# Linear attention: the queries' products taken one head at a time over 64 rows, instead of two heads at once through a block-diagonal matrix

## Chip, core and metric

The kernel runs on one core of a Trainium2 chip. The metric is the device time of one execution in microseconds (us); of the kernel before, the median of three runs is 1168.2 us. Names of engines in the rows: PE is TensorE's products, PEld its loads of the fixed operand ("weights"), DVE is VectorE, ACT is ScalarE, POOL is GpSimd, SPq the queue on which SyncE issues transfers.

## What is computed

```python
# attention: batch 4, heads 8, sequence 576, head size 64, all float32
q_s = softmax(q over the head size)          # per query
k_s = softmax(k over the sequence)           # per column of a head
kv  = einsum('bhsd,bhse->bhde', k_s, v)      # one 64 x 64 matrix per batch and head
x   = einsum('bhsd,bhde->bhse', q_s, kv)     # 2304 tokens of 8 x 64 = 512
# first mixture: 8 experts, each token goes to one, 288 tokens per expert, best logits first
logits = x @ w_gate                          # 512 -> 8
...                                          # greedy assignment, then relu(x @ w1[e]) @ w2[e]
# second mixture: 4 experts, all tokens through all, weighted by normalised domain_probs
out += p[:, e:e+1] * (relu(x @ w1[e]) @ w2[e])
```

## The kernel before

The program has three stages. The first, some 93 us, is the attention with the gate's logits. The second searches for one expert after the other which 288 tokens it takes, gathers them from `x_rows` in memory and runs them through the expert; the third is the second mixture. In each stage the calls are collected in a `Plan`; every engine's instructions are then issued in an order that the plan works out from prices (`price`, L107), from the dependences and from a priority (L190 to L197). On the chip each engine runs its list in that order and waits where an operand is not ready. An engine never passes over an instruction that waits.

The attention stage has 8 steps `kv_half` (L588: a batch and four of its eight heads) and 18 chunks of 128 queries: 16 from `q_half` (L655), whose queries are of one batch, and 2 from `q_rest` (L662), of which each holds the last 64 queries of two batches. The order of the steps stands in `ATT["order"]` (L67).

`kv_half` adds up in the PSUM tile `pkv` the products of exp(k) and v for pairs of heads; head `h` of a pair goes to partitions 64h to 64h+63, and a 65th column holds the column sum. DVE divides and writes the two heads into `mov`, a matrix of 128 rows and 146 columns for each pair: head 0 in rows 0 to 63 and columns 0 to 63, head 1 in rows 64 to 127 and columns 64 to 127, zeros beside them, two columns of ones that give the queries' sums, and 16 columns for the gate. For the gate's columns the block is transposed into the tile `pg`, copied to `kvT` by ACT, multiplied by `wg` (the gate's weights) and copied back into `mov` by DVE.

`q_cols` (L617) transposes a chunk's queries (tile `pa`, four transposes), takes exp of them (`qT`, ACT), and multiplies each pair's 128 columns of `qT` by that pair's `mov`:

```python
xp = aps("pkv", [P, 2, 512], F32, 2).rearrange("p a (b c) -> p (a b) c", b=2)
for p in range(NP):
    for rs, b in parts:
        pl.tensor.matmul(xp[rs, p, :146], qT[:, p, rs], mov[b][:, p], start=True, stop=True)
```

The first operand of `matmul` behind the output is the fixed one (a load of weights), the second is streamed through it. The results are divided by the sums (`rq`), the gate's part is added to `logits`, and the 512 outputs (`xo`) go to `x_rows`, on DVE straight from PSUM or, by `ATT["x"]`, copied by ACT (`xr`) and multiplied on POOL.

After the last chunk, the first search (`search`, L339) reads `logits`, and the second stage goes on from there.

Of the kernel before, what the change touches and what calls it, by code (L numbers as in the profile page):

```python
# [8 lines left out]
F32 = mybir.dt.float32  # L9
# [4 lines left out]
AF = mybir.ActivationFunctionType  # L14
# [11 lines left out]
SM = P * NI  # L26
SR = S - SM
NC = NT // P

DL = (650.0, 1300.0, 330.0, 1900.0)  # L30
GRP = ((0, 12), (12, 18))
# [57 lines left out]
class Plan:  # L89
# [16 lines left out]
    @staticmethod  # L106
    def price(key, name, out, ins):  # L107
        n = 1
        for c in out.shape[1:]:
            n *= c  # L110
        m = n
        for i in ins:
            c = 1
            for d in i.shape[1:]:
                c *= d
            m = max(m, c)
        if "dma" in name:
            return (1000.0 if key == "POOL" else 60.0, 4 * n * out.shape[0])
        if key == "PE":
            if name == "transpose":  # L120
                return 110.0
            d = ins[1].dtype
            if d == F32:
                return 85.0 if n == D + 1 else max(n, 128) * 1.7 if n >= 96 else 213.0
            if d == F32R:
                return n / 2.4 + 3
            return max(27.0, n / 2.4 + 3)
        if key == "DVE":
            if name == "tensor_reduce":
                return 70 + 1.04 * m  # L130
            if name == "tensor_scalar" or name == "tensor_copy":
                rate = 0.52 if str(ins[0].space).endswith("SB") and str(out.space).endswith("SB") else 1.04
                return 68 + rate * n + (60 if len(ins) > 1 else 0)
            rate = 0.52 if out.dtype == BF and name == "tensor_tensor" else 1.04
            return 69 + (60 if name == "scalar_tensor_tensor" and len(ins) > 2 else 0) + rate * n
        if key == "ACT":
            return 55 + 0.835 * n
        if key == "POOL":
            if name == "tensor_tensor":
                return 155 + 2.1 * n  # L140
            return 180 + 1.05 * n
        return 60.0
# [99 lines left out]
def block_kernel(ctx, tc, q, k, v, w_gate, m1_w1, m1_w2, probs, m2_w1, m2_w2, out):  # L242
# [19 lines left out]
    nc.gpsimd.iota(dpc, pattern=[[1, P]], base=0, channel_multiplier=-1)  # L262
    ident = const.tile([P, P], F32, name="ident")
    nc.vector.tensor_scalar(ident, dpc, 0.0, None, op0=OP.is_equal)
    wg = const.tile([P, NP, E1], F32, name="wg")
    logits = const.tile([P, NC, E1], F32, name="logits")

    pl = Plan(nc)
# [201 lines left out]
    with ExitStack() as at:  # L470
# [22 lines left out]
        for nm, bp in (("k", 0), ("v", 0), ("q", 0), ("k", 1), ("v", 1), ("q", 1)):  # L493
            src = {"k": k, "v": v, "q": q}[nm]
            for b in (2 * bp, 2 * bp + 1):
                load_main(nm, src, b, 2 if nm == "k" and b == 0 else 1)
                if b == 2 * bp:
                    load_rest(nm, src, bp)
            if bp == 0 and nm == "v":
                pl.sync.dma_start(wg, w_gate.rearrange("(c p) e -> p c e", p=P))  # L500
        for b in range(B):
            pl.sync.dma_start(pr[:, b * NI:(b + 1) * NI], probs[b * S:b * S + SM].rearrange("(r i) e -> r i e", i=NI))
            s = b % 2
# [6 lines left out]
            pl.gpsimd.memset(va[(1 - s) * SR:(2 - s) * SR, NI], 0.0)  # L510
            vaug.append(va)
        for b in range(B):
            mov[b] = kt_(f"mov{b}", [P, NP, 146])
            pl.gpsimd.memset(mov[b], 0.0)
            for s in range(2):
                pl.gpsimd.memset(mov[b][s * D:(s + 1) * D, :, 128 + s:129 + s], 1.0)
        ps = kt_("ps", [P, NC])
        px = kt_("px", [P, NC, EX])
        HH = H // 2
# [62 lines left out]
        def guard(o, t, way):  # L582
            if way:
                pl.scalar.activation(o, t, AF.Copy, bias=EPS)
            else:
                pl.vector.tensor_scalar(o, t, EPS, None, op0=OP.add)

        def kv_half(bp, u, s):  # L588
            b = 2 * bp + s
            kx, ke, va = tiles["k", "x", bp], kt_(f"ke{s}", [P, NI, H, D]), vaug[s]  # L590
            kv = aps("pkv", [P, 2, 512], F32, 2)[:, 0, :HP * (D + 1)].rearrange("p (a c) -> p a c", a=HP)
            for j in range(HP):
                for i in range(NI + 1):
                    for h in range(2):
                        n = 2 * (u * HP + j) + h
                        w = ke[:, i, n] if i < NI else kx[:, n]
                        pl.tensor.matmul(kv[h * D:(h + 1) * D, j], w, va[:, i, n], start=(i == 0), stop=(i == NI))
            rs = kt_("rs", [P, HP, 1], F32, 2)
            guard(rs, kv[:, :, D:], ATT["g"][0])
            pl.vector.reciprocal(rs, rs)  # L600
            mv = mov[b][:, u * HP:(u + 1) * HP]
            for h in range(2):
                hp = slice(h * D, (h + 1) * D)
                pl.vector.tensor_tensor(mv[hp, :, hp], kv[hp, :, :D], rs[hp].to_broadcast([D, HP, D]), op=OP.mult)
            tp = aps("pg", [P, 512])
            for j in range(HP):
                pl.tensor.transpose(tp[:, j * P:(j + 1) * P], mv[:, j, :P], ident)
            kvT = kt_("kvT", [P, HP, P], F32, 2)
            pl.scalar.activation(kvT, tp[:, :HP * P].rearrange("p (a b) -> p a b", a=HP), AF.Copy)
            g = tp[:, 384:384 + HP * E1].rearrange("p (a e) -> p a e", a=HP)  # L610
            for j in range(HP):
                pl.tensor.matmul(g[:, j], kvT[:, j], wg[:, u * HP + j], start=True, stop=True)
            for h in range(2):
                hp = slice(h * D, (h + 1) * D)
                pl.vector.tensor_copy(mv[hp, :, 130 + 8 * h:138 + 8 * h], g[hp])

        def q_cols(qt, c, parts):  # L617

# [2 lines left out]
                pl.tensor.transpose(tp[:, p], qt[:, 2 * p:2 * p + 2, :], ident)  # L621
            qT = kt_("qT", [P, NP, P], F32, 2)
            pl.scalar.activation(qT, tp, AF.Exp)
            xp = aps("pkv", [P, 2, 512], F32, 2).rearrange("p a (b c) -> p (a b) c", b=2)
            for p in range(NP):
                for rs, b in parts:
                    pl.tensor.matmul(xp[rs, p, :146], qT[:, p, rs], mov[b][:, p], start=True, stop=True)
            rq = kt_("rq", [P, NP, 2], F32, 2)
            guard(rq, xp[:, :, 128:130], ATT["g"][1])
            pl.vector.reciprocal(rq, rq)  # L630
            lp = kt_("lp", [P, NP, 2, E1], F32, 2)
            pl.vector.tensor_tensor(lp, xp[:, :, 130:146].rearrange("p a (h e) -> p a h e", h=2),
                                    rq[:, :, :, None].to_broadcast([P, NP, 2, E1]), op=OP.mult)
            xo = kt_("xo", [P, DX], F32, 3)
            eng, xv = pl.vector, xp[:, :, :P]
            if ATT["x"][c]:
                xr = kt_("xr", [P, NP, P], F32, 2)
                pl.scalar.activation(xr, xv, AF.Copy)
                eng, xv = pl.gpsimd, xr
            eng.tensor_tensor(xo[:, :DM].rearrange("p (a h d) -> p a h d", a=NP, h=2),  # L640
                              xv.rearrange("p a (h d) -> p a h d", h=2),
                              rq[:, :, :, None].to_broadcast([P, NP, 2, D]), op=OP.mult)
            pl.vector.tensor_reduce(logits[:, c], lp.rearrange("p a h e -> p e (a h)"), axis=AX.X, op=OP.add)
            pl.scalar.activation(xo[:, DM:], px[:, c], AF.Copy)
# [391 lines left out]
```

## Time and profile before

| what | value |
|---|---|
| three runs | 1166.06, 1168.2, 1171.34 us (median 1168.2) |
| the profiled execution | 1172.77 us, of which its span (first to last instruction) is 1170.9 us |
| TensorE's products, busy | 1099.8 us, 94% of the span |
| DVE, ACT, POOL, busy | 713.1, 470.9 and 500.1 us |
| mean granted TensorE clock | 0.977 of full speed |

The three runs lie within 0.45% of each other, and the profiled execution is 0.4% above their median. A busy share is an average over stages with different limits, so the stage of the change has to be looked at by itself. A product of two float32 operands leaves two records in the trace, each with a load of its own; a transpose on TensorE leaves one. A record's duration goes from its start to its modelled end and overlaps the next one, so what a product costs the engine is read from the distance between records.

### The profile page before, as it was taken

The page shows a single profiled execution, that of the slowest core. Times are in us where ns is not written, and L with a number is a line of the kernel's source. Part 1 is how long each engine was busy: PE and PEld are TensorE (multiplying, and loading weights), DVE is VectorE, ACT ScalarE, POOL GpSimd, SP SyncE. Part 2 cuts the span into 40 slices and gives each one's busy share as a digit, 9 for nine tenths or more (in the row PEclk, how much of TensorE's full clock was granted, in tenths as well). Part 3 has the DMA queues.
Part 4 walks back from the last instruction along what each step waited for, and adds up shares of the span by engine and source line. Part 5 has one row for each costly group of instructions (what it writes and reads, how often), then busy time and mean ns, then how long its engine had stood idle before and what let it go on. Part 6 is the DMA issues. An engine that isn't in the chain of part 4 may idle for free.

```text
span 1170.9 us, 20079 instructions
## 1 busy us (share of the span) xinstructions
PE 1099.8 (94%) x7708; PEld 989.4 (84%) x7708; DVE 713.1 (61%) x1700; ACT 470.9 (40%) x945; POOL 500.1 (43%) x645
## 2 busy tenths in 40 slices
PE   4783999999999899999999999999999999999996
PEld 2673888999989899889989898798899898888995
DVE  5977575877744565555555559755555555555553
ACT  3451354645556543333434344433333333333321
POOL 5462111211121666555455555945344343444222
PEclk9896798999999999999999999999999999999998
DMA  9922686877788512111111112202111111110001
GB/s 278 236 92 87 168 241 155 218 203 189 204 229 222 155 38 72 55 54 37 55 54 55 55 37 72 89 24 69 36 37 37 55 36 36 54 38 18 1 37 54
DMA packets 81760, 113.64 MB, mean 97 GB/s; under 512 B 11520, under 2 KB 56576, under 8 KB 81664
## 3 DMA queue, kind: packets, MB, share of 16 engines
q1 hardware_dynamic: 74080, 86.09, 24.1%
q0 software_dynamic: 7584, 26.27, 10.2%
q8 instruction: 60, 0.98, 0.3%
q14 instruction: 36, 0.29, 0.1%
HBM read 86.08 MB, written 9.48 MB: 82 GB/s over the span
## 4 chain that ended last, share of the span: by engine, by line
PE 79%; DVE 7%; DMA 5%; issue 4%; POOL 3%; ACT 1%; SPq 0%; DVEq 0%; POOLq 0%; ACTq 0%
PE o L85 31%; PE x L85 16%; PE z L85 8%; PE y L85 7%; PE hp L85 7%; PE q L85 4%; DMA w<-raw 2%; DMA xg<-x_rows,idx 2%; PE pkv L85 2%; PE sm L85 2%; PE tp L85 1%; PE pm L85 1%; DVE yops L85 1%; POOL w L85 1%; DMA k<-in_k 1%
## 5 line engine op out<-in xcount | busy, mean ns | idle before, releaser
L85 PE MATMUL o<-w,h 128*128 128x512 f32 x1728 | 534.8, 394 | 4.4 <-DVE h L85 2.8
L85 PEld LDWEIGHTS o<-w,h 128*128 128x128 f32 x1728 | 311.1, 188 | 48.4 <-DVE h L85 4.2
L85 PE MATMUL x<-yops,w 128*128 128x256 f32 (+1 forms) x1536 | 342.9, 295 | 0.6 <-ACT yops L85 0.6
L85 POOL TENSOR_TENSOR w<-raw,w 128x256 fp32r<-128x256 f32 x224 | 171.4, 795 | 312.9 <-ACT w L85 267.7
L85 DVE SCALAR_TENSOR_TENSOR y<-o,prs,y 128x512 f32<-128x512 f32 x270 | 198.7, 748 | 142.6 <-PE o L85 140.0
L85 PEld LDWEIGHTS x<-yops,w 128*128 128x128 f32 x1536 | 262.6, 188 | 21.6 <-ACT yops L85 0.8
L85 ACT ACTIVATE w<-raw 128x1024 fp32r<-128x1024 f32 (+2 forms) x192 | 166.2, 878 | 192.6 <-PE q L85 66.8
L85 PE MATMUL z<-yops,w 128*128 128x256 f32 (+1 forms) x768 | 178.3, 295 | 0.7 <-DVE mid L85 0.7
L85 ACT ACTIVATE mid<-x 128x256 f32<-128x256 f32 (+1 forms) x192 | 78.0, 408 | 206.0 <-PE x L85 203.9
L85 DVE SCALAR_TENSOR_TENSOR h<-mid,h 128x256 fp32r<-128x256 f32 (+1 forms) x192 | 117.1, 610 | 64.7 <-ACT h L85 64.4
L85 ACT ACTIVATE h<-mid 128x256 fp32r<-128x256 f32 (+1 forms) x192 | 84.6, 441 | 139.6 <-DVE mid L85 139.4
L85 PEld LDWEIGHTS z<-yops,w 128*128 128x128 f32 x768 | 132.9, 189 | 5.8 <-DVE mid L85 0.9
L85 PE MATMUL y<-h,w 128*128 128x288 f32 x768 | 127.6, 306 | 1.5 <-DMA w<-raw 0.9
L85 PE MATMUL hp<-xT,w 128*128 128x288 f32 x768 | 126.6, 306 | 0.4 <-ACT xT L85 0.4
L85 PEld LDWEIGHTS y<-h,w 128*128 128x128 f32 x768 | 109.1, 192 | 3.6 <-DMA w<-raw 1.8
L85 POOL DMA_DIRECT2D w<-raw x32 | 28.9, 903 | 192.4 <-ACT h L85 81.9
L85 PEld LDWEIGHTS hp<-xT,w 128*128 128x128 f32 x768 | 109.4, 193 | 1.8 <-ACT xT L85 0.6
L85 POOL TENSOR_TENSOR w<-sums,w 128x256 fp32r<-128x256 f32 x128 | 100.5, 821 | 23.1 <-ACT w L85 23.1
L85 PE MATMUL q<-yops,w 128*128 128x256 f32 (+1 forms) x384 | 102.5, 295 | 0.0
L85 PEld LDWEIGHTS q<-yops,w 128*128 128x128 f32 x384 | 70.8, 188 | 7.5
L85 DVE TENSOR_TENSOR mid<-mid,z 128x256 f32<-128x256 f32 (+1 forms) x128 | 57.6, 450 | 30.1 <-PE z L85 17.5
L85 DVE TENSOR_TENSOR mid<-mid,q 128x256 f32<-128x256 f32 (+1 forms) x64 | 29.0, 453 | 53.5 <-PE q L85 46.4
(198 smaller groups left out, 1011.4 us busy)
## 6 DMA issues: line engine op xcount, KB each, us to landing
raw<-in_moe_w SPq DMA_DIRECT2D x128, 512.0 KB, 3.8
w<-raw POOLq DMA_DIRECT2D x32, 512.0 KB, 5.8
x_rows<-xo SPq DMA_DIRECT2D x16, 258.5 KB, 2.4
v<-in_v SPq DMA_DIRECT2D x4, 1024.0 KB, 9.6
q<-in_q SPq DMA_DIRECT2D x4, 1024.0 KB, 11.1
k<-in_k SPq DMA_DIRECT2D x3, 1024.0 KB, 9.6
k<-in_k SPq DMA_DIRECT2D x2, 512.0 KB, 6.0
x_rows<-xo SPq DMA_DIRECT2D x4, 129.2 KB, 2.7
```

Of the source, the lines that this page charges most:

```text
L85: lambda: getattr(self.engine, name)(*args, **kw), ins, out, kw.get("start", True))
```

## The change

One head's product now has 64 rows of its own on both sides. `mov` keeps, for each pair of heads, head 0 in rows 0 to 63 and head 1 in rows 64 to 127 of the same 73 columns (64 of the head, one of ones, eight of the gate); the zeros are gone. In `q_cols` each pair is two products of 64 contracted rows and 73 columns; those of head 0 go to one PSUM bank, those of head 1 to the other. In `kv_half` one DVE instruction over 128 partitions takes the place of two over 64, in the division and in the copy of the gate's columns. The block is transposed from 64 columns, so `kvT` has 64 partitions, and the gate's product is two products of 64 by 64. `wg` is laid out with 64 rows. `price` gives the new products 85 ns each, as it gave those of `kv_half`.

```diff
 NC = NT // P
+QC = D + 1 + 8
...
-                return 85.0 if n == D + 1 else max(n, 128) * 1.7 if n >= 96 else 213.0
+                return 85.0 if n == D + 1 or n == QC and ins[0].shape[0] == D else max(n, 128) * 1.7 if n >= 96 else 213.0
...
-    wg = const.tile([P, NP, E1], F32, name="wg")
+    wg = const.tile([D, H, E1], F32, name="wg")
...
-                pl.sync.dma_start(wg, w_gate.rearrange("(c p) e -> p c e", p=P))
+                pl.sync.dma_start(wg, w_gate.rearrange("(h d) e -> d h e", d=D))
...
-            mov[b] = kt_(f"mov{b}", [P, NP, 146])
-            pl.gpsimd.memset(mov[b], 0.0)
-            for s in range(2):
-                pl.gpsimd.memset(mov[b][s * D:(s + 1) * D, :, 128 + s:129 + s], 1.0)
+            mov[b] = kt_(f"mov{b}", [P, NP, QC])
+            pl.gpsimd.memset(mov[b][:, :, D:D + 1], 1.0)
...
-            for h in range(2):
-                hp = slice(h * D, (h + 1) * D)
-                pl.vector.tensor_tensor(mv[hp, :, hp], kv[hp, :, :D], rs[hp].to_broadcast([D, HP, D]), op=OP.mult)
+            pl.vector.tensor_tensor(mv[:, :, :D], kv[:, :, :D], rs.to_broadcast([P, HP, D]), op=OP.mult)
             tp = aps("pg", [P, 512])
             for j in range(HP):
-                pl.tensor.transpose(tp[:, j * P:(j + 1) * P], mv[:, j, :P], ident)
-            kvT = kt_("kvT", [P, HP, P], F32, 2)
-            pl.scalar.activation(kvT, tp[:, :HP * P].rearrange("p (a b) -> p a b", a=HP), AF.Copy)
+                pl.tensor.transpose(tp[:D, j * P:(j + 1) * P], mv[:, j, :D], ident)
+            kvT = kt_("kvT", [D, HP, P], F32, 2)
+            pl.scalar.activation(kvT, tp[:D, :HP * P].rearrange("p (a b) -> p a b", a=HP), AF.Copy)
             g = tp[:, 384:384 + HP * E1].rearrange("p (a e) -> p a e", a=HP)
             for j in range(HP):
-                pl.tensor.matmul(g[:, j], kvT[:, j], wg[:, u * HP + j], start=True, stop=True)
-            for h in range(2):
-                hp = slice(h * D, (h + 1) * D)
-                pl.vector.tensor_copy(mv[hp, :, 130 + 8 * h:138 + 8 * h], g[hp])
+                for h in range(2):
+                    hp = slice(h * D, (h + 1) * D)
+                    pl.tensor.matmul(g[hp, j], kvT[:, j, hp], wg[:, 2 * (u * HP + j) + h], start=True, stop=True)
+            pl.vector.tensor_copy(mv[:, :, D + 1:], g)
...
-            xp = aps("pkv", [P, 2, 512], F32, 2).rearrange("p a (b c) -> p (a b) c", b=2)
+            xp = aps("pkv", [P, 2, 512], F32, 2)[:, :, :NP * QC].rearrange("p h (a c) -> p a h c", a=NP)
             for p in range(NP):
                 for rs, b in parts:
-                    pl.tensor.matmul(xp[rs, p, :146], qT[:, p, rs], mov[b][:, p], start=True, stop=True)
+                    for h in range(2):
+                        hp = slice(h * D, (h + 1) * D)
+                        pl.tensor.matmul(xp[rs, p, h], qT[hp, p, rs], mov[b][hp, p], start=True, stop=True)
```

The reads of `xp` behind these lines (`rq`, `lp`, `xr`, `xo`) follow the new layout with as many elements as before.

Since prices and pieces differ, the plan issues the attention stage in another order. From the first search on, all engines have the same order as before. A product uses a part of TensorE's array: by the rows that it contracts (128, or half of them) and by the partitions that it writes (128, or half of them). In what follows this is the shape of a product, and going from one shape to another a switch. A transpose of 64 columns writes 64 partitions, so it has the shape of the products in `kv_half`. In the stage before, from its first product to the first search, PE's list has 41 switches between two shapes (128 rows to 128 partitions, 128 rows to 64), the last one into the search; in the changed one it has 86, between four shapes. The rows below are of PE's list: output, streamed operand and fixed operand, then partitions and columns of the output, and how many stand in a row.

First place: PE's last chunks ahead of the first search, before.

```order
L85 MATMUL pa_147<-ident,qe_157 128x128
L85 MATMUL pkv_137<-mov_0_122,qT_148 128x146 x4
L85 MATMUL pa_147<-ident,qe_157 128x128 x3
L85 MATMUL pkv_141<-mov_0_122,qT_153 128x146 x4
L85 MATMUL pa_152<-ident,qe_157 128x128 x4
L85 MATMUL pkv_137<-mov_0_123,qT_148 128x146 x4
L85 MATMUL pkv_141<-mov_0_123,qT_153 128x146 x4
```

Here all rows have one shape: transposes (`pa`) and products (`pkv`) use the whole array. The same place after the change:

```order
L86 MATMUL pa_152<-ident,qe_145 128x128 x4
L86 MATMUL pkv_137<-mov_0_123,qT_148 128x73 x8
L86 MATMUL pkv_141<-mov_0_123,qT_153 128x73 x8
L86 MATMUL pa_147<-ident,qe_157 128x128 x4
L86 MATMUL pkv_137<-mov_0_122,qT_148 128x73 x8
L86 MATMUL pa_152<-ident,qe_157 128x128 x4
L86 MATMUL pkv_141<-mov_0_122,qT_153 128x73 x8
L86 MATMUL pkv_137<-mov_0_123,qT_148 128x73 x8
L86 MATMUL pkv_141<-mov_0_123,qT_153 128x73 x8
```

Each group of products of 128x73 contracts 64 rows, so it has a shape of its own: these nine rows have five switches where the seven rows above have none, and three chunks stand at the end without a transpose between them, where there were two.

Second place: PE's list around the last `kv_half`, whose block is transposed (`pg<-ident`) and multiplied by the gate's weights (`pg<-wg`), before.

```order
L85 MATMUL pg_139<-ident,mov_0_123 128x128 x2
L85 MATMUL pkv_141<-mov_0_122,qT_153 128x146 x4
L85 MATMUL pkv_137<-mov_0_122,qT_148 128x146 x4
L85 MATMUL pa_152<-ident,qe_145 128x128 x4
L85 MATMUL pg_139<-wg,kvT_143 128x8
L85 MATMUL pa_147<-ident,qe_157 128x128 x4
L85 MATMUL pg_139<-wg,kvT_143 128x8
L85 MATMUL pkv_141<-mov_0_122,qT_153 64x146
```

Until the last row, where a rest chunk begins, nothing switches. The same place after the change:

```order
L86 MATMUL pg_139<-ident,mov_0_123 64x128 x2
L86 MATMUL pa_152<-ident,qe_145 128x128 x3
L86 MATMUL pkv_141<-mov_0_122,qT_153 128x73 x8
L86 MATMUL pa_152<-ident,qe_145 128x128
L86 MATMUL pa_147<-ident,qe_157 128x128 x3
L86 MATMUL pg_139<-wg,kvT_143 64x8 x2
L86 MATMUL pkv_137<-mov_0_122,qT_148 128x73 x8
L86 MATMUL pa_147<-ident,qe_157 128x128
L86 MATMUL pg_139<-wg,kvT_143 64x8 x2
L86 MATMUL pkv_141<-mov_0_122,qT_153 64x73 x2
```

The gate's products (64 rows to 64 partitions) now stand between transposes of the whole array and chunks of 64 rows, and there are seven switches where there was one.

## Rows read from the trace of the kernel before

**Rows 1.** The page: span, and part 1 (busy us, share of the span, instructions).
```profile
span 1170.9 us, 20079 instructions
PE 1099.8 (94%) x7708; PEld 989.4 (84%) x7708; DVE 713.1 (61%) x1700; ACT 470.9 (40%) x945; POOL 500.1 (43%) x645
```

**Rows 2.** Busy time by stretch: span, engines (instructions), granted clock, DMA share, GB/s.
```profile
20.00:60.00 40.00, 32.63 (x361) 27.26 (x361) 35.33 (x79) 19.58 (x47) 19.53 (x17) 0.91 0.95 237
60.00:91.00 31.00, 26.46 (x269) 23.16 (x268) 25.02 (x77) 17.98 (x56) 20.28 (x16) 1.00 0.29 98
```

**Rows 3.** Timeline of SyncE's queue: start us, us, what is issued.
```profile
47.43 4.17 SPq L85 DMA_DIRECT2D qx<-in_q  x2
51.73 42.21 SPq L85 DMA_DIRECT2D x_rows<-xo  x20
110.21 1.01 SPq L866 DMA_DIRECT2D raw<-in_moe_w  x2
```

**Rows 4.** Chain that ended last, 60 to 92.7 us: start us, us, engine, tile.
```profile
62.66 0.29 DVE mov L85
...
65.75 0.19 DVE mov L85
...
69.33 0.19 DVE mov L85
...
70.28 0.31 DVE mov L85
...
71.68 1.32 PE pkv L85 x40
...
75.64 0.59 PE pa L85 x4
...
83.48 0.44 PE pa L85 x4
...
88.16 1.01 PE pkv L85 x8
...
89.90 1.24 PE pkv L85 x8
```

**Rows 5.** Groups by shape, PE, 73.0 to 91.2 us: count, busy us, mean ns.
```profile
L85 PE MATMUL pkv<-mov,qT 128*128 128x146 f32 x68 | 10.2, 294 | 0.9 <-ACT xo L85 0.7
L85 PE MATMUL pa<-ident,qe 128*128 128x128 f32 x32 | 4.9, 277 | 0.0
L85 PE MATMUL pkv<-mov,qT 128*64 128x146 f32 x32 | 3.0, 300 | 0.0
L85 PE MATMUL pg<-wg,kvT 128*128 128x8 f32 x8 | 1.2, 238 | 0.0
```

**Rows 6.** Timeline of PE's weight loads, with the idle time ahead of a row.
```profile
64.06 0.53 PEld L85 LDWEIGHTS pg<-wg,kvT 128*128 128x128 f32 x4
...
71.61 0.55 PEld L85 LDWEIGHTS pkv<-va,ke 128*64 128x64 f32 x16 [0.17 <-issue]
...
75.57 0.42 PEld L85 LDWEIGHTS pa<-ident,qe 128*128 128x128 f32 x4 [0.20 <-issue]
```

**Rows 7.** Groups by shape, weight loads, 60 to 91 us.
```profile
L85 PEld LDWEIGHTS pg<-wg,kvT 128*128 128x128 f32 x16 | 2.2, 191 | 0.1
```

**Rows 8.** Timeline of PE's products: start us, us, what.
```profile
68.01 0.64 PE L85 MATMUL pkv<-va,ke 128*64 128x65 f32 x16
68.48 0.29 PE L85 MATMUL pkv<-va,kx 128*64 128x65 f32 x4
```

**Rows 9.** Groups by shape, 0 to 260 us, the writers of `mov`.
```profile
L85 DVE TENSOR_TENSOR mov<-pkv,rs 64x128 f32<-64x128 f32 x16 | 4.6, 287 | 0.6
...
L85 DVE COPY mov<-pg 64x16 f32<-64x16 f32 x16 | 2.7, 170 | 0.6 <-PE pg L85 0.5
```

**Rows 10.** Busy time by stretch, as in rows 2, in a shorter one.
```profile
42.00:48.00 6.00, 5.01 (x23) 4.99 (x24) 4.97 (x16) 2.73 (x11) 1.71 (x2) 0.50 1.11 314
```

More of the change, by code (lines that the diff above doesn't have):

```diff
@@ L623, in q_cols @@
             pl.scalar.activation(qT, tp, AF.Exp)
-            xp = aps("pkv", [P, 2, 512], F32, 2).rearrange("p a (b c) -> p (a b) c", b=2)
+            xp = aps("pkv", [P, 2, 512], F32, 2)[:, :, :NP * QC].rearrange("p h (a c) -> p a h c", a=NP)
             for p in range(NP):
                 for rs, b in parts:
-                    pl.tensor.matmul(xp[rs, p, :146], qT[:, p, rs], mov[b][:, p], start=True, stop=True)
+                    for h in range(2):
+                        hp = slice(h * D, (h + 1) * D)
+                        pl.tensor.matmul(xp[rs, p, h], qT[hp, p, rs], mov[b][hp, p], start=True, stop=True)
             rq = kt_("rq", [P, NP, 2], F32, 2)
-            guard(rq, xp[:, :, 128:130], ATT["g"][1])
+            guard(rq, xp[:, :, :, D], ATT["g"][1])
             pl.vector.reciprocal(rq, rq)
             lp = kt_("lp", [P, NP, 2, E1], F32, 2)
-            pl.vector.tensor_tensor(lp, xp[:, :, 130:146].rearrange("p a (h e) -> p a h e", h=2),
+            pl.vector.tensor_tensor(lp, xp[:, :, :, D + 1:],
                                     rq[:, :, :, None].to_broadcast([P, NP, 2, E1]), op=OP.mult)
             xo = kt_("xo", [P, DX], F32, 3)
-            eng, xv = pl.vector, xp[:, :, :P]
+            eng, xv = pl.vector, xp[:, :, :, :D]
             if ATT["x"][c]:
-                xr = kt_("xr", [P, NP, P], F32, 2)
+                xr = kt_("xr", [P, NP, 2, D], F32, 2)
                 pl.scalar.activation(xr, xv, AF.Copy)
@@ L640, in q_cols @@
             eng.tensor_tensor(xo[:, :DM].rearrange("p (a h d) -> p a h d", a=NP, h=2),
-                              xv.rearrange("p a (h d) -> p a h d", h=2),
+                              xv,
                               rq[:, :, :, None].to_broadcast([P, NP, 2, D]), op=OP.mult)
```

## The prediction, made before the run

> **What bounds the kernel now.** The page comes first [rows 1]: TensorE is busy for 94% of the span. That says nothing of the change, which lies in the first 93 of 1171 us, so I read that stage alone. From 20 to 60 us [rows 2] the DMA engines are 0.95 busy and DVE for 35.3 of 40 us; PE has 7.4 us to spare. From 60 to 91 us [rows 2] the DMA share is 0.29: the last queries are issued by 51.6 us, and after that SyncE's queue holds only the stores of finished chunks [rows 3]. So up to some 60 us the stage follows its loads and DVE, and then it works off what is left. The chain of waits says who sets the pace there [rows 4]: from 60 to 71 us it runs over DVE (four of its pieces are second halves of writes to `mov`), and from 71.7 us over PE without much else, to the last chunk's products, which end at 91.1 us (89.90 and 1.24). The search and the loads of the first expert's weights (110.2 us) [rows 3] follow the end of this stage, and from the first search on no engine's order differs. So a microsecond at the end of the attention is one at the end of the kernel, and nothing behind it changes.
>
> **The products of a chunk.** Before, a chunk takes 8 records in 1.01 us [rows 4], 0.126 us for a record of 146 streamed columns. After, it has 16 records of 73 columns. The streaming of one would be half, 0.063 us. But each has its own load of 128 weight columns, and the gate's products show what a record costs when next to nothing is streamed: four loads of 128 columns in 0.53 us [rows 6], each lasting 0.19 [rows 7], so they start (0.53 - 0.19) / 3 = 0.113 us apart. Loads of 128 columns thus end last, not the streaming. What saves the change is overlap: the products of `kv_half`, which write two different halves of the partitions, show that two halves of the array work at the same time. Sixteen of their records start within 68.48 - 68.01 = 0.47 us [rows 8], 0.029 each, or 0.059 for a pair that streams 65 columns and loads 64 each. No row shows two halves of the rows doing this. I take it that they do, as the two halves of the columns do, with a pair of records every 0.113 us: 8 pairs make a chunk of 0.90 us in place of 1.01. The window from 73.0 us, after the last `kv_half`'s sums, to 91.2 us holds 68 such records [rows 5], 8.5 chunks, and the changed order has 8.5 after the same place: -0.9 us. The bounds: at the 0.059 of rows 8, 68 pairs take 4.0 instead of 8.6 us, -4.6; with no overlap, 136 records at 0.113 take 15.4, +6.8.
>
> The Trainium skill ("TensorE: Matmul & The Clock Gate", section LDWEIGHTS) says that a load's time goes by its columns and not by its rows, some 107 ns for 128. The 0.113 us of rows 6 and 7 agree for 128 rows; for 64 no run shows it. By that figure a chunk would be 0.86 us, as an estimate.
>
> **The rest chunks** take 3.0 us in that window [rows 5], about 0.6 of it four switches (below), so 2.4. After, they are 64 records over a quarter of the array each; at 0.029 they take 1.9: -0.5. Bounds -1.0 (three of four at once) and +1.4 (0.059 a record, half as much overlap).
>
> **The gate's products**: 8 records in the window [rows 5] at 0.113 are 0.9 us; after, 16 records of half as many weight columns on two halves of the partitions, at 0.029, 0.5: -0.4, bounds -0.4 and 0.
>
> **Switches of shape.** This speaks against the change. The four transposes at 75.64 us, which follow products of half the partitions, take 0.59 us on the chain; the four at 83.48, which follow the whole array, 0.44 [rows 4]. A switch costs 0.15 us. The loads show why: they sit idle for 0.17 and 0.20 us ahead of the first one in the new shape, waiting for nothing that the profile names [rows 6]; elsewhere they run ahead of the products. In the window the list before has 8 switches, the search's included, the changed one 18: +10 x 0.15 = +1.5 us. Bounds: +1.0 (a few fall into waits for `qT`) and +2.0 (0.20 each, since the first load of 128 columns lies open longer than one of 64).
>
> The Trainium skill ("TensorEngine Tiling (Array Packing)", Key Properties) says that a change of tiling mode drains TensorE. The idle loads of rows 6 agree.
>
> **The window together**: -0.9 - 0.5 - 0.4 + 1.5 = -0.3 us.
>
> **What comes ahead of it.** DVE writes `mov` with 16 instructions of 287 ns and copies the gate's columns with 16 of 170 [rows 9]; after, 8 of each over all partitions with as many elements in a partition, so -8 x 0.457 = -3.7 us of DVE. On the chain from 60 to 71 us the second halves are 0.29 + 0.19 + 0.19 + 0.31 = 1.0 us [rows 4]: -1.0. Before 60 us fall five of the divisions and four of the copies, 2.1 us, on an engine that is busy for 88% but also waits for loads: I take half, -1.05 (bounds 0 and -2.1). Against that stand PE's other switches, 86 - 18 - (41 - 8) = 35 more, 5.2 us, less what it saves there: 7.5 chunks at 0.1, and six gates at 0.2, together 2. That is 3.2 us more for an engine that has 7.4 idle up to 60 us. The gate and its transposes lie between two DVE steps, so not all of it is hidden: I take half, +1.6 (bounds 0 and +3.2). Together -0.45.
>
> The rest is nothing: ACT's copies (`kvT`, `xr`, `rq`) keep their elements per partition, and ACT has 13 of 31 us idle [rows 2]; POOL's clearing of `mov` goes away in the first microseconds, before its first data; `wg` is one transfer as before.
>
> **Sum**: -0.3 - 0.45 = -0.75 us on the profiled 1172.8 us, so 1172.0 there; that execution lies 4.6 us above the median of 1168.2, so **1167.4 us**. A measurement of this kernel can tell some 0.5%, 5.8 us, from no change.
>
> **Rivals.** *The halves of the rows don't overlap.* Loads and products of 64 rows then queue one behind the other. In the window the chunks cost +6.8 instead of -0.9 and the rests +1.4 instead of -0.5; ahead of it 7.5 chunks take 60 records' worth of 0.113 twice, +6.8 more on PE, of which half is on the path as above. That is -0.75 + 7.7 + 1.9 + 3.4 = +12 us, 1180 us. It decides as soon as a pair of records takes over some 0.17 us, where the window's 68 pairs lose 3 us. For it: no row has two row halves at work, and the loads are what binds. Against it: the column halves overlap fully.
>
> *A load of 64 rows is as quick as one of 64 columns.* Then pairs come every 0.06 us and the window's chunks fall by 4.6. Not all of it arrives, since DVE, busy for 25.0 of 31 us [rows 2], is next: of its 6 idle us I let 3 go. With 1 us more ahead of the window: -0.75 - 3 - 1, 1163.4 us. For it: half the data in each load. Against it: nothing in the rows.
>
> *The clock.* From 42 to 48 us TensorE was granted 0.50 of full speed, its lower level [rows 10], after a stretch in which it had waited often; from 60 to 91 us it had 1.00 [rows 2]. More gaps at the switches could bring a second such stretch into the window, which would stretch some 3.4 us of work to 6.8: 1171 us.
>
> *The change does nothing it says*: the two heads go to the array as before and only the order changes. The order alone moves the end by a chunk or two, about 1 us, which is within the forecast.
>
> **How the numbers follow.** The forecast (overlap, load-bound, switches take it back) has 0.55; adding its terms' bounds where they are independent, it spans 1163.5 to 1172. No overlap 0.22, fast loads 0.15, the clock 0.08. Faster by over 0.5% (below 1162.4): the better third of fast loads, and orders that fall well beyond my bounds, 0.15. Slower (above 1174.0): no overlap, and the clock together with bad switches, 0.24. Within 0.5%: 0.61. The range, 1162 to 1179, takes in the fast loads and part of the missing overlap.
>
> **What will show it.** Right: chunks of 16 records in 0.9 us, pairs of loads 0.11 apart; four transposes behind a chunk in 0.59 instead of 0.44 us; idle loads put down to "issue" about twice as often; half as many DVE writes of `mov`; the last chunk's products ending within 2 us of 91.1. Wrong: a chunk of 1.8 us or of 0.5; a switch that costs 0.05 or 0.3 us; an end of the stage that the end of the kernel doesn't follow.

## The result and the profile after

The changed kernel takes 1183.4 us (median of six runs, 1177.7 to 1189.0); the kernel before takes 1169.5 beside it. The ratio is 1.0116, with a 95% interval of 1.0092 to 1.0140: slower, and outside the range given. The profiled execution takes 1181.6 us. Page, span and part 1, as in [rows 1]:

```profile
span 1179.9 us, 20440 instructions
PE 1115.7 (95%) x7900; PEld 1000.0 (85%) x7900; DVE 708.6 (60%) x1684; ACT 470.4 (40%) x945; POOL 493.1 (42%) x637
```

Busy time by stretch: span, PE, PEld, DVE, ACT, POOL (instructions), granted clock, DMA share, GB/s. The first two answer to [rows 2]; the last two are stretches at the lower clock.

```profile
20.00:60.00 40.00, 35.21 (x317) 27.69 (x316) 27.69 (x62) 16.52 (x40) 18.11 (x16) 0.71 0.98 236
60.00:91.00 31.00, 30.71 (x387) 25.52 (x388) 16.31 (x46) 14.27 (x42) 16.57 (x13) 0.83 0.13 47
36.60:63.90 27.30, 27.09 (x218) 21.35 (x218) 15.76 (x47) 9.83 (x26) 8.37 (x8) 0.50 0.85 213
77.50:84.30 6.80, 6.80 (x68) 5.60 (x68) 1.29 (x7) 1.58 (x5) 3.18 (x3) 0.50 0.24 92
```

The roles are exchanged. Before, DVE was busy for 35.3 of the 40 us from 20 to 60 us and PE had 7.4 to spare; now PE has 4.8 to spare there and 0.3 of the next 31, while DVE waits. The granted clock says why: ahead of 91 us TensorE was at 0.50, its lower level of 1.2 GHz, for 27.3 + 6.8 = 34.1 us, where before it was for 6.8 us around [rows 10]. In both stretches PE was busy almost all the time; it did not want for work. The six runs differ in the same way: the shortest span, 1175.4 us, has a mean clock of 0.968, the longest, 1187.1, of 0.957.

Chain that ended last, at five places, and two rows of the timeline of PE's products between them:

```profile
45.20 1.06 PE pkv L86 x8
...
58.13 1.91 PE pkv L86 x8
...
87.03 1.12 PE pkv L86 x16
88.15 0.59 PE pa L86 x4
...
94.11 2.01 PE pkv L86 x32
```

```profile
65.81 1.11 PE L86 MATMUL pkv<-mov,qT 64*128 64x73 f32 x8
67.97 1.11 PE L86 MATMUL pkv<-mov,qT 64*128 64x73 f32 x8
```

A chunk is 16 records. At 87 and 94 us, at the full clock, it takes 1.12 and 1.00 us, about as much as before (1.01, [rows 4]). At 45.20, at half the clock, half a chunk takes 1.06. The rows at 58.13, 65.81 and 67.97 are another thing: eight records, half a chunk, take 1.91 us at half and 1.11 at full clock, twice their share. These are four products of one head behind each other. `kv_half` uses only the first bank of `pkv`, so the bank of head 1 is free earlier, and the plan issues head 1's products as soon as they can go and head 0's later. In PE's list four of the 16 whole chunks stand like this (the first expectations below say five), and part of a rest chunk.

The loss builds up early. The sums of the last `kv_half` end at 83.5 us instead of 73.0 (+10.5), the last chunk's products at 104.2 instead of 91.1 (+13.1), and the first expert's weights are issued here:

```profile
123.57 1.00 SPq L865 DMA_DIRECT2D raw<-in_moe_w  x2
```

That is 13.4 us later than in [rows 3]. The last chunk has a share of its own in this. From 101.4 us on TensorE is at 0.50 again, for 41.0 us; before, such a stretch begins at 96.4 us, behind the last chunk, and lasts 34.1. So the last chunk, side by side, takes 1.98 us here where the one at 87.03 takes 1.12. Timeline of PE's products:

```profile
102.17 1.98 PE L86 MATMUL pkv<-mov,qT 64*128 64x73 f32 x16 [1.77 <-DVE sg L86]
```

The span is 9.0 us longer, 4.4 less than the first expert's load is late. Most of the difference goes at one place, from 185 to 195 us of the profiled execution before: the changed kernel's products are 12.3 us late just ahead of it and 7.4 just behind. There the kernel before waited 2.2 us for a gather and then was at 0.50 for 6.8 us; at the same place the changed one waited 0.2 us and had the full clock. Waits of PE and busy time by stretch, before and then after:

```profile
PE tp L85 <- DMA xg<-x_rows,idx: 2.4, 2, 2.2
188.60:195.40 6.80, 6.09 (x26) 5.78 (x26) 2.19 (x7) 1.33 (x3) 0.00 (x0) 0.50 0.54 152
```

```profile
PE tp L86 <- DMA xg<-x_rows,idx: 0.2, 1, 0.2
188.00:205.00 17.00, 16.79 (x174) 15.18 (x174) 12.13 (x49) 8.28 (x13) 4.97 (x6) 1.00 0.78 205
```

These are two single executions. The medians are 13.8 us apart, about as much as the load is late.

### The profile page after: what moved, and what is told of

Read it like the earlier page. It is cut to its first block, busy times and chain, and to the rows that moved or that the text cites. A ratio compares the mean times of both kernels' runs of the same rounds, so it can differ in the third digit from the quotient of the medians.

```text
span 1179.9 us, 20440 instructions
## 1 busy us (share of the span) xinstructions
PE 1115.7 (95%) x7900; PEld 1000.0 (85%) x7900; DVE 708.6 (60%) x1684; ACT 470.4 (40%) x945; POOL 493.1 (42%) x637
## 4 chain that ended last, share of the span: by engine, by line
PE 84%; DVE 6%; DMA 3%; issue 3%; POOL 2%; ACT 1%; SPq 0%; DVEq 0%; POOLq 0%; ACTq 0%
PE o L86 31%; PE x L86 16%; PE y L86 8%; PE z L86 8%; PE hp L86 8%; PE q L86 4%; PE pkv L86 4%; DMA xg<-x_rows,idx 2%; PE sm L86 2%; PE pm L86 1%; PE tp L86 1%; POOL w L86 1%; DVE yops L86 1%; DMA k<-in_k 1%; POOL out L931 1%
## 5 line engine op out<-in xcount | busy, mean ns | idle before, releaser
L86 DVE SCALAR_TENSOR_TENSOR h<-mid,h 128x256 fp32r<-128x256 f32 (+1 forms) x192 | 117.5, 613 | 64.7 <-ACT h L86 63.2
L86 PE MATMUL y<-h,w 128*128 128x288 f32 x768 | 125.1, 303 | 1.7 <-DVE h L86 1.4
```

The source lines that it names most:

```text
L86: lambda: getattr(self.engine, name)(*args, **kw), ins, out, kw.get("start", True))
```

## The experiments

Theory A: the lower clock takes the time. Theory B: the order does, by the products of one head without a neighbour of the other. Theory C: the switches of shape.

The kernels were run in five groups, the result's among them, in which the kernel before has medians of 1168.4 to 1171.2 us. Each ratio is taken against the kernel before of its own group, so kernels of different groups are better compared by their ratios than by their medians.

**Heads side by side, and what else it could be.** *Pairs*: the two products of a pair become one entry of the plan.

```diff
-                    for h in range(2):
-                        hp = slice(h * D, (h + 1) * D)
-                        pl.tensor.matmul(xp[rs, p, h], qT[hp, p, rs], mov[b][hp, p], start=True, stop=True)
+                    def pair(p=p, rs=rs, b=b):
+                        for h in range(2):
+                            hp = slice(h * D, (h + 1) * D)
+                            nc.tensor.matmul(xp[rs, p, h], qT[hp, p, rs], mov[b][hp, p], start=True, stop=True)
+                    pl.add("PE", 170.0, pair, [qT[:, p, rs], mov[b][:, p]], [xp[rs, p, 0], xp[rs, p, 1]])
```

> The changed kernel, but the two heads' products of a pair are one entry of the plan, so they always stand next to each other. Theory A (the clock: thin streams over part of the array and the many gaps keep TensorE at its lower level longer, and that is the loss): products side by side fill both halves of the rows, the low stretch from 36.6 to 63.9 us gets shorter, and the time follows the clock: 1168 to 1176 us. Theory B (the order alone: four or more products of one head stand together in 5 of the 16 whole chunks, and such a chunk takes 1.8 us instead of 0.9 at the full clock): 5 x 0.9 = 4.5 us come back whatever the clock does, 8 or 9 if these chunks fall into the low stretch: 1175 to 1179. Theory C (the 45 additional switches of shape): there are 82 left of 86, so within 1 us of the changed kernel, 1182.

Measured: 1174.1 us, ratio 1.0033 (1.0014 to 1.0051). Most of the loss is gone, but this edit changes the whole order, so it can't be put down to the neighbours alone.

*Quarters*: the queries of a pair are halved too, so that four products of 64 rows and 64 queries stand together in one entry.

```diff
+                        for rs, b in quarters:
+                            for h in range(2):
+                                hp = slice(h * D, (h + 1) * D)
+                                nc.tensor.matmul(xp[rs, p, h], qT[hp, p, rs], mov[b][hp, p], start=True, stop=True)
```

> The changed kernel with each pair's products split once more by queries, so that four products of 64 rows to 64 partitions stand together, one entry of the plan. The trace of the changed kernel has 30 records of such quarter products in 0.90 us of its rest chunks, less their length some 0.021 us a record, so a chunk of 32 would take 0.7 us instead of 0.9, and the loads are of 64 columns. A (clock): the whole array is in use, so the low stretch shortens as with the pairs or more: 1164 to 1174 us. B (order): as the pairs, less 16 x 0.2 = 3 us: 1171 to 1176. C (switches, 76 left): 1179 to 1181.

Measured: 1170.7 us, ratio 0.9997 (0.9981 to 1.0014): as the kernel before. It is at 0.50 for 23.9 us ahead of 91 us, not much less than the changed kernel, so a clock that is low for longer than before can be made up for elsewhere. In its chain a chunk takes less time:

```profile
84.67 0.72 PE pkv L628 x32
```

*The kernel before with two products of 73 columns*, over all 128 rows, in place of one of 146; and *the kernel before with 32 more switches*, by one more transpose of 64 columns in each chunk:

```diff
-                    pl.tensor.matmul(xp[rs, p, :146], qT[:, p, rs], mov[b][:, p], start=True, stop=True)
+                        for c in (slice(0, 73), slice(73, 146)):
+                            nc.tensor.matmul(xp[rs, p, c], qT[:, p, rs], mov[b][:, p, c], start=True, stop=True)
```

```diff
+                    if p == NP - 1:
+                        nc.tensor.transpose(tp[:D, p], qt[:, 2 * p, :], ident)
```

> The kernel before, its order kept, but each product of 146 columns is made of two of 73 columns over all 128 rows, each with its own load. A chunk's 16 records of 128-column loads then take 16 x 0.113 = 1.8 us instead of 1.0 at the full clock, with no additional switch of shape and all rows in use. If only the direct cost counts, the 8.5 chunks of the last window give +6.8 us and those before it about half of 6.8: 1178 to 1181. A (clock, by how much is streamed rather than by how many rows are used): the low stretch from 41.8 to 48.6 us gets longer too, and the time goes to 1182 or more. If it is the use of half the rows that keeps the clock down, the low stretch stays at one or two of its lengths here.

> The kernel before with one more transpose at the end of each chunk's four, of 64 columns, which writes again what is already there: 18 records of 0.11 us and up to 36 switches of shape in and out. Direct cost if PE sets the pace everywhere: 18 x (0.11 + 2 x 0.15) = 7.4 us; 9 chunks lie in the last window, so at least 3.3: 1172 to 1177. C (switches as the cause): the low stretch of the clock gets as long as in the changed kernel, and the time goes to 1178 to 1185. A and B: the clock's low stretch stays as before.

Measured: 1181.1 us for the first, ratio 1.0086 (1.0055 to 1.0118), and 1172.1 for the second, 1.0007 (0.9984 to 1.0030). In the first a chunk of 16 records over all rows takes 1.74 us in its chain:

```profile
94.03 1.74 PE pkv L629 x16
```

That is 0.109 us a record, the price of a load. It is the prediction's first rival acted out, and costs about what that was to cost. The switches cost nothing that can be measured: C is out as the main cause. These are switches between all and half of the written partitions; switches to half of the rows were not tried by themselves.

**What starts the low clock?** In the changed kernel the clock falls at 36.6 us, just as TensorE has waited 1.92 us. Timeline of DVE there, and PE's transposes that waited:

```profile
34.75 1.92 DVE L86 TENSOR_TENSOR m<-m 128x256 f32<-128x256 f32 x1
36.59 0.16 DVE L86 COPY mov<-pg 128x16 f32<-128x16 f32 x1
```

```profile
36.80 0.42 PE L86 MATMUL pg<-ident,mov 128*64 128x128 f32 x1 [1.92 <-DVE mov L86]
```

Since `mov` is written by one instruction instead of two, the plan found room for `m<-m` ahead of the copy; before it stood behind. Two kernels exchange just these, in the changed kernel and in the one before. `m` and `c` are their places in the plan's order:

```diff
+            order.remove(m)
+            order.insert(order.index(c) + 1, m)
```

```diff
+            order.remove(m)
+            order.insert(order.index(c), m)
```

A third moves, in the changed kernel's order, each product next to the other head's, and nothing else, by which 8 of the 86 switches go too; a fourth has both edits.

```diff
+        for i in self.marks.get("p", []):
+            first, last = sorted((i, i + 1), key=order.index)
+            order.remove(first)
+            order.insert(order.index(last), first)
```

> The changed kernel with one DVE instruction moved: the reduction m<-m of 128x256 that stands ahead of the copy mov<-pg of the first block now stands behind it; all else is in the same order. In the changed kernel this m<-m takes 1.92 us, the copy ends at 36.75 us, and TensorE's transposes of the second block wait 1.92 us for it, with ready sums behind them; the clock falls to 0.50 at 36.6 us. Theory A (the wait starts the stretch of low clock, and the low clock costs the time): the wait falls to under 0.5 us, the low stretch before 64 us shrinks from 27 us to 7 to 15 us, and the kernel takes 1174 to 1179 us instead of 1183.4. Theory B (the order of the products alone): the wait lies in a part with slack; 1182 to 1184 us. If the clock falls anyway, at some other gap, within 42 us, the wait is not its cause.

> The kernel before with the same two things in the changed kernel's order: m<-m ahead of the two copies of the first block; all else as before, products over 128 rows too. Theory A: TensorE waits some 1.3 us longer at 35 us, the clock falls at 36 to 38 us instead of 41.8 and stays low for 15 us or more, and the kernel takes 1173 to 1178 us. Theory B: 1169 to 1171 us, as before. If the wait comes and the clock does not fall, the low clock needs the thinner products as well.

> The changed kernel's order with one thing moved: in the chunks whose products of one head stand together, each such product is moved next to the other head's (4 chunks and a few of a rest chunk); all else in the same order. Theory B (products of one row half behind each other do not overlap): 4 chunks of 1.8 to 2.2 us become 0.9 to 1.1, and the kernel takes 1172 to 1177 us. Theory A: TensorE gets less busy, the clock stays as low as before, and most of the saved time is not seen: 1180 to 1183 us.

> The two edits of the changed kernel together: m<-m behind the copy, and the products of one head next to the other head's. Theory A and B both hold and add up: 1168 to 1172 us. Only A: as the kernel with m<-m moved alone, within 1.5 us. Only B: as the kernel with the products moved alone, within 1.5 us.

Measured: 1185.5 us for the changed kernel with `m<-m` moved, ratio 1.0116 (1.0087 to 1.0146), just what the changed kernel has; 1172.5 for the kernel before with the exchange, 1.0011 (0.9987 to 1.0035); 1178.5 with the heads side by side, 1.0069 (1.0044 to 1.0095); 1180.8 with both, 1.0079 (1.0054 to 1.0104). So the neighbours are worth 1183.4 - 1178.5 = 4.9 us (0.47% by the ratios; 1185.5 - 1180.8 = 4.7 us with `m<-m` moved in both), and this wait nothing that can be told: theory A in this form fell. How much of the 4.9 us comes by the clock stays open: in the profiled execution it is at 0.50 for 3.4 us less. With `m<-m` moved, the wait only moved to the next block, the clock fell at 38.3 us instead, and a later stretch was longer. Timeline of PE's products, then busy time by stretch, of the kernel with `m<-m` moved:

```profile
38.60 0.63 PE L86 MATMUL pg<-ident,mov 128*64 128x128 f32 x2 [1.51 <-DVE mov L86]
```

```profile
72.40:99.70 27.30, 27.16 (x242) 22.75 (x241) 9.32 (x30) 8.83 (x29) 10.17 (x9) 0.50 0.18 59
```

Here PE was busy for 27.16 of 27.30 us, and stayed at 0.50. In the kernel before with the exchange the clock fell early too, at 37.9 us instead of 41.8, with PE just as busy behind it, but it was back after 10.2 us, and low once more from 65.2 to 75.5 us. This execution is 4.0 us above the median of its kernel. Busy time by stretch:

```profile
37.90:48.10 10.20, 10.20 (x71) 9.14 (x68) 7.21 (x27) 2.21 (x10) 2.52 (x2) 0.50 1.06 293
```

So not what started the low clock was the thing to change, but what the engine did in it. That is theory A': TensorE is busy, but with products that stream few columns over half of the rows.

**Wider products.** Each product of 64 rows streams 128 columns instead of 73: `mov` is padded with 55 columns of ones, whose results nobody reads. It is more work and takes nothing away; the orders stay (but for one DVE instruction in the first microseconds).

```diff
+QW = 128
...
-            mov[b] = kt_(f"mov{b}", [P, NP, QC])
-            pl.gpsimd.memset(mov[b][:, :, D:D + 1], 1.0)
+            mov[b] = kt_(f"mov{b}", [P, NP, QW])
+            pl.gpsimd.memset(mov[b][:, :, D:], 1.0)
...
-            xp = aps("pkv", [P, 2, 512], F32, 2)[:, :, :NP * QC].rearrange("p h (a c) -> p a h c", a=NP)
+            xp = aps("pkv", [P, 2, 512], F32, 2)[:, :, :NP * QW].rearrange("p h (a c) -> p a h c", a=NP)
```

The same was done to the pairs and to the kernel with the heads side by side. Later came a control, with this layout but products of 73 columns, and a step at 100 columns (the product's operands end at `:QC` and at `:100`).

> The changed kernel with each product of 64 rows streaming 128 columns instead of 73 (55 columns of ones, whose results nobody reads); TensorE's order, DVE's but for one swap in the first microseconds, ACT's and the loads are the same. A pair of products has two loads of 128 columns, 0.1116 us apart at full clock, and 146 columns took 0.126 us in the kernel before, so 128 columns should stay about as quick. Theory A' (TensorE is busy but its thin streams do not bring the clock back, and this is what the changed kernel loses beside the order of heads): the stretches of 0.50 before 100 us shrink from 34 us to under 20 us, and the kernel takes 1172 to 1178 us instead of 1183.4. Theory B (only products without a neighbour of the other half cost): 1183 to 1186 us.

> The same widening in the kernel whose two heads of a pair are one entry (1174.1 us). Theory A': the stretch of 0.50 from 38.2 to 62.1 us gets shorter than 15 us and the kernel takes 1167 to 1171 us. Without A': 1174 to 1177 us.

> The same widening in the changed kernel's order with the products of the two heads side by side (1178.5 us). Theory A': 1168 to 1173 us, since both losses are gone. Without A': 1178 to 1181 us.

> Control of the widening: the changed kernel with mov and the PSUM tile laid out for 128 columns and filled as there, all engines' orders as there, but each product streaming its 73 columns. If the columns streamed are what the wide kernel gained by (theory A'), this one is as slow as the changed kernel, 1181 to 1185 us, with stretches of 0.50 of 27 us or more before 100 us. If the layout or the order of the first microseconds did it, it takes 1175 to 1178 us.

> The wide kernel at 100 streamed columns, between 73 (1183.4 us) and 128 (1176.6 us), all orders the same. Theory A' makes the time fall with the columns: 1178 to 1182 us and stretches of 0.50 before 100 us between 20 and 34 us. Else as at 73 columns.

| products, in the order of | columns | median us | ratio (95%) | at 0.50, stretches that begin ahead of 94 us, profiled run |
|---|---|---|---|---|
| changed kernel | 73 | 1183.4 | 1.0116 (1.0092 to 1.0140) | 34.1 us |
| control, padded | 73 | 1187.1 | 1.0166 (1.0128 to 1.0204) | 47.8 us |
| padded | 100 | 1179.8 | 1.0094 (1.0062 to 1.0125) | 34.1 us |
| padded | 128 | 1176.6 | 1.0053 (1.0035 to 1.0072) | 20.5 us |
| heads side by side | 73 | 1178.5 | 1.0069 (1.0044 to 1.0095) | 30.7 us |
| heads side by side | 128 | 1174.8 | 1.0033 (1.0014 to 1.0052) | 17.0 us |
| pairs | 73 | 1174.1 | 1.0033 (1.0014 to 1.0051) | 23.9 us |
| pairs | 128 | 1171.8 | 1.0011 (0.9995 to 1.0027) | 13.7 us |

Busy time by stretch of the control, of 100 and of 128 columns, in this order:

```profile
66.00:100.00 34.00, 33.40 (x344) 28.11 (x344) 15.64 (x46) 13.88 (x43) 16.98 (x13) 0.70 0.17 58
```

```profile
66.00:100.00 34.00, 32.30 (x418) 26.86 (x415) 19.01 (x59) 17.32 (x54) 18.02 (x14) 0.94 0.24 80
```

```profile
66.00:100.00 34.00, 30.51 (x412) 25.36 (x410) 19.83 (x67) 17.79 (x57) 17.94 (x15) 1.00 0.27 88
```

With 75% more columns streamed the kernel is 6.8 us quicker than the changed one and 10.5 quicker than its control (0.6% and 1.1% by the ratios). The granted clock of the stretch goes 0.70, 0.94, 1.00, and the records done in it 344, 418, 412, while the orders are the same. But this stretch alone shows too much: the changed kernel itself has 0.90 and 411 records in it,

```profile
66.00:100.00 34.00, 32.48 (x411) 27.55 (x411) 17.82 (x56) 16.86 (x54) 18.01 (x14) 0.90 0.24 80
```

and at 100 columns the clock is at 0.50 from 35.6 to 66.4 us, mostly ahead of it, and for 3.4 us later, which makes 34.1 us, as in the changed kernel. All runs together say it better than one execution of each: their mean granted clock is 0.955 to 0.961 for the control, 0.957 to 0.968 for the changed kernel, 0.965 to 0.970 at 100 columns and 0.972 to 0.976 at 128. Streaming more can save time in no way but the clock that I can name, so for the columns A' is shown in this kernel.

The layout isn't the cause, since the control has it, and that one is rather slower than the changed kernel. The wide pairs and the wide kernel with the heads side by side came out 0.8 and 1.8 us above what was expected, so A' and the neighbours aren't all. And the two overlap: the neighbours are worth 4.9 us at 73 columns, but 1176.6 - 1174.8 = 1.8 at 128.

**Half of the rows, in the order of before.** In the kernel before, the products contract 64 of the 128 rows only, 146 columns and all orders kept; head 1 is left out of the result.

```diff
-                    pl.tensor.matmul(xp[rs, p, :146], qT[:, p, rs], mov[b][:, p], start=True, stop=True)
+                        nc.tensor.matmul(xp[rs, p, :146], qT[:D, p, rs], mov[b][:D, p], start=True, stop=True)
```

> The kernel before, in its own order, with the products contracting only 64 of the 128 rows (head 1 is left out of the result); loads of 128 columns, 146 columns streamed, as many records as before. A product then has another shape than the transposes beside it, some 30 more switches, which cost next to nothing in the control with 36 switches. Theory A' in the form that rows at work count: the clock falls for longer than 6.8 us before 93 us, by 10 us or more, and the kernel takes 1174 to 1180 us. If only the columns streamed count: 1170 to 1173 us and the clock as before.

Measured: 1175.2 us, ratio 1.0043 (1.0025 to 1.0062). The clock is at 0.50 from 44.2 to 64.7 us, 20.5 instead of 6.8. But not all of the 4.8 us is the clock: at the full clock a chunk takes 0.18 us more than before,

```profile
92.04 1.19 PE pkv L628 x8
```

and the transposes behind it have a switch. So this run shows that fewer rows, with the same list, go with a longer stretch at the lower level; it gives no price for it.

**Transposes over 65 columns**, to bring the block's transposes back to the shape of the whole array, in the wide pairs and in the quarters:

```diff
-                pl.tensor.transpose(tp[:D, j * P:(j + 1) * P], mv[:, j, :D], ident)
+                pl.tensor.transpose(tp[:D + 1, j * P:(j + 1) * P], mv[:, j, :D + 1], ident)
```

> The kernel with a pair's two heads as one entry and 128 streamed columns (1171.8 us), with the transposes of mov over 65 columns instead of 64, so that they write more than half of the partitions and have the shape of the whole array again. If the rest of its loss is the half-sized transposes (thin work again), the first stretch of 0.50 (13.7 us) gets shorter and it takes 1168 to 1171 us; if not, 1171 to 1173 us.

> The kernel with four products of 64 rows and 64 queries for each pair (1170.7 us), with the transposes of mov over 65 columns. If the transposes' shape keeps the clock up: 1166 to 1169 us, faster than the kernel before. If not: 1170 to 1172 us.

Measured: 1173.7 us, 1.0040 (1.0016 to 1.0063), and 1170.1, 1.0015 (0.9993 to 1.0038). No gain; the half-sized transposes aren't what is left. No version tried is faster than the kernel before.

## Why the prediction was wrong

**The step on the clock failed.** The prediction gave the lower clock 0.08, as one second stretch of 6.8 us in the last window that costs 3.4 us. It took the stretch of [rows 10] as a matter of waits and gaps. In fact it was 34.1 us ahead of 91 us with PE busy throughout, and the last chunk besides. The products' price was worked out at the full clock alone, and nobody asked what the engine is granted when every product works with half of the rows and half of the columns. What wider streams give back of this is 6.8 us; what the 20.5 us that stay at 0.50 cost is not shown.

**The step on overlap was right and then used where it doesn't hold.** The two row halves do overlap, load-bound: the pairs of the chunk at 87.03 us start 0.112 us apart (87.200, 87.312, 87.424), for a forecast of 0.113, and a chunk of 16 records with the switch ahead of it takes 1.00 to 1.12 us. But the prediction wrote that "8 pairs make a chunk of 0.90 us" for all of them and did not read in the changed list whose products stand side by side. Four chunks have no neighbours of the other half, and cost double, as its first rival said of all: 4.9 us, by the kernel that only moves them. That this rival's 1180 us lies near the 1183.4 measured is luck, since 12 of the 16 whole chunks do overlap. What queues there is one load behind the other: in the rows at 65.81 and 67.97 the records are 0.111 to 0.113 us apart behind the first two, about the 0.113 us of the loads alone in [rows 6]. They stay 0.111 to 0.112 apart in the kernel that streams 128 columns:

```profile
64.56 1.16 PE L87 MATMUL pkv<-mov,qT 64*128 64x128 f32 x8
```

The Trainium skill ("TensorE: Matmul & The Clock Gate", Part 3, The mechanism) says that a load overlaps products under way only where it goes to another group of rows, and that products keep their order. That side by side is quicker agrees; the "only" does not, since 55 more columns streamed add nothing from record to record within one half.

**"What comes ahead of it" had the wrong engine.** It put +3.2 us of PE into 7.4 us of idle time and expected DVE's savings to arrive, for -0.45 in all. The sums of the last `kv_half` end 10.5 us later. DVE's instructions did become 8 and 8, at 290 and 171 ns; but PE, at half the clock, took DVE's place as the bound, and what DVE saved lies in its idle time:

```profile
L86 DVE TENSOR_TENSOR mov<-pkv,rs 128x128 f32<-128x128 f32 x8 | 2.3, 290 | 0.5
L86 DVE COPY mov<-pg 128x16 f32<-128x16 f32 x8 | 1.4, 171 | 2.9 <-PE pg L86 1.6 <-ACT kvT L86 1.2
```

**The switches** have the forecast price where they can be seen (four transposes in 0.59 us at 88.15). As a term they were too dear rather than too cheap, as far as can be told: 32 of them in the kernel before cost 0.07%, at most 0.3%, and 32 x 0.15 would be 0.4%.

**The end of the stage** is followed by the end of the kernel about one to one, as the prediction held, if the medians are taken: the first expert's load is 13.4 us late, and they are 13.8 apart. In the two profiled executions 9.0 are left at the end, by the wait and the stretch at 0.50 that only the one of the kernel before has.

The parts make up more than half of it. Side by side and wide, the kernel takes 1174.8 us, 8.6 less than the changed one; some 4 to 5 us stay against the kernel before. It is still at 0.50 for 17 us there. The pairs, wide, in another order, are within 0.5% of before and at 0.50 for 13.7 us. How the rest divides between the clock that is still low, the order and the gate's smaller products stays open.

## What to carry to other kernels

Cost a change that makes TensorE's products smaller at both levels of its clock, and look in the stage itself for stretches at 0.50 in which PE is busy: there, more work in each product can be quicker. Where products of two row halves are to overlap, read in the issued order that they stand next to each other, and tie them together where a scheduler could part them. A saving on an engine is worth nothing when the same change makes another one the bound.

## What the runs showed of the hardware

In two executions a DVE instruction with two operands in SBUF waited for GpSimd's, whenever it began. Away from it, `m<-m` takes 0.43 us. Timeline of DVE in the changed kernel:

```profile
40.49 0.43 DVE L86 TENSOR_TENSOR m<-m 128x256 f32<-128x256 f32 x1
```

At 35 us it ran beside GpSimd's `qe<-q,qm`. Timeline of POOL in the changed kernel, then of POOL and of DVE in the kernel before with the exchange:

```profile
34.20 2.19 POOL L86 TENSOR_TENSOR qe<-q,qm 128x1024 f32<-128x1024 f32 x1 [1.10 <-DMA pr<-in_moe_domain_probs]
```

```profile
34.24 2.19 POOL L85 TENSOR_TENSOR qe<-q,qm 128x1024 f32<-128x1024 f32 x1 [1.10 <-DMA kx<-in_k]
```

```profile
35.31 1.40 DVE L85 TENSOR_TENSOR m<-m 128x256 f32<-128x256 f32 x1
```

It began at 34.75 us (shown above) and at 35.31 and ended both times 0.28 us after GpSimd did (36.67 against 36.39, 36.71 against 36.43), so its 1.92 and 1.40 us are mostly waiting. The Trainium skill ("SBUF — State Buffer", SBUF: two separate sides) says that a DVE instruction with two SBUF inputs and GpSimd share a pair of ports, held for a whole instruction; the trace agrees, but for the last 0.28 us, which are less than the 0.43 that `m<-m` takes by itself.

A product that streams 128 columns was as quick as one that streams 73, where its load of 128 columns binds. A chunk in the chain of the widened kernel, for 1.12 us in the changed one:

```profile
93.89 1.11 PE pkv L87 x16
```
